# ScalarE alone reads the first layer's banks, and VectorE squares the even tile in SBUF

## The chip, the cores and the metric

The kernel runs on one core of a Trainium2 chip. The core has a matrix engine (TensorE, PE in the profile; its weight loads are listed as PEld), three engines for elementwise work (VectorE or DVE, ScalarE or ACT, GpSimd or POOL) and SyncE (SP), which here only issues DMAs. Matrix results land in PSUM, 8 banks of 128 partitions by 512 float32 values; everything else lies in SBUF. Each engine runs its own instructions in the order in which they were written and waits on semaphores that the others raise. The metric is the time of one execution on the device in microseconds (us), the median of several runs.

## The reference

Three layers follow one another. The first filters each of 8 batches (3072 by 256) in the frequency domain; the second is a feed-forward layer with a squared ReLU, 256 to 2048 to 256; the third is a soft mixture of 8 experts, of which every slot's input is a softmax over all 24576 tokens.

```python
y = np.fft.irfft(np.fft.rfft(x, axis=1) * F, n=x.shape[1], axis=1)   # per batch

h = np.maximum(x @ w_in, 0.0)
x = h * h @ w_out

logits = x @ phi
d = softmax over tokens of logits;  slot_input = d.T @ x
slot_out[e] = np.maximum(slot_input[e] @ w1[e], 0.0) @ w2[e]
out = (softmax over slots of logits) @ slot_out
```

The term that this case is about is `h * h` with `h = max(x @ w_in, 0)`: 24576 by 2048 values, computed in 768 tiles of 128 by 512.

## The kernel before

All weights of the first layer stay in SBUF, split in a high and a low part (`wiH`, `wiL`). The 24576 tokens go through in 48 chunks of 512 (`CH`), and each chunk's 2048 features in 8 pairs of 128-feature tiles, so the main loop has 384 pairs, P = 0 to 383. A pair has an even tile (k = 0, PSUM bank `p0`) and an odd tile (k = 1, bank `p1`). `layer` writes a tile with six matmuls (lines 382 to 384, twice): the three products of a split multiplication, for two halves of the inner dimension. There is one bank of each kind, so the first matmul of the next pair's even tile cannot begin before whoever reads `p0` is done with it; the same holds for `p1`.

`square` takes a tile from PSUM and leaves its squared ReLU in an SBUF tile `h` (tags `h0` and `h1`, four buffers each). The two kinds of tile go different ways. For the even tile ScalarE writes a scaled ReLU to `h` (line 390) and VectorE then reads the bank a second time and multiplies, `max(p, 0) * h` (line 391). [...]

VectorE then transposes each tile in blocks of 32 (`turn_h`, line 401, into `hT`), and PE multiplies `h` of four tiles by the product of the second layer's weights and `phi` into the chunk's logits in bank `L` (`logit`, line 410, called for P - 3 at each odd P). When a chunk's logits are complete, a chain runs beside the pairs of the following chunk. ScalarE and VectorE move the logits to SBUF (`evac_l`, lines 447 and 448), PE spreads them (`gather`, lines 455 and 456, bank X), VectorE takes the maximum (`emax`, lines 461 to 464), ScalarE the exponential (`expo`, line 470), VectorE transposes that into `eT` (`turn_e`, line 487) and the logits into `lt` (`turn_l`, line 481, four instructions), and PE then adds the chunk to the slots (`slot_in`, line 508, 128 matmuls into four banks), which VectorE accumulates (`accum`, line 524).

The frequency filter of the next batch is woven into the same loop: matmuls `mm_a` (lines 142 to 144), `mm_b` (188) and `mm_g` (221); between the last two VectorE multiplies by the filter (`filt`, line 199, four instructions) and GpSimd joins the parts (`join`, line 208, four instructions). GpSimd also makes the low parts of split tiles (lines 131 and 348).

The order on every engine is the order in which the Python code is called. `pair` emits one pair, and between its quarters `run_streams` calls those side steps whose due time has come and for which enough of the five side banks are free. `side` takes the bank that has been free the longest, and `done` puts a bank back at the end of that list. Nothing is reordered later; semaphores between engines are put in for every true dependence and every reuse of a buffer.

Of the kernel before, what the change touches and what calls it, by code (L numbers as in the profile page):

```python
# [9 lines left out]
ACTF = mybir.ActivationFunctionType  # L10
ALU = mybir.AluOpType
# [27 lines left out]
def body(tc, x, cA, cAf, fwd, inv, flt, cst, w_in, w_out, phi, w1, w2, out):  # L39
    nc = tc.nc  # L40
    sync = nc.sync
    act, vec, gps, pe = nc.scalar, nc.vector, nc.gpsimd, nc.tensor
# [343 lines left out]
    def square(P, k):  # L386
        p = h2[P, k]
        h = h2[P, k] = G["mlp"].tile([128, CH], F32, tag=f"h{k}", name="h", bufs=4)
        if k == 0:
            act.activation(out=h, in_=p, func=ACTF.Relu, scale=2.0 ** -16)  # L390
            vec.scalar_tensor_tensor(out=h, in0=p, scalar=0.0, in1=h, op0=ALU.max, op1=ALU.mult)  # L391
        else:
            act.activation(out=h, in_=p, func=ACTF.Relu, scale=2.0 ** -8)  # L393
            gps.tensor_tensor(out=h, in0=h, in1=h, op=ALU.mult)  # L394

    def turn_h(P, k):

# [17 lines left out]
    def pair(P):  # L415
        live = P < NP
        for k in range(4):
            t = 2 * P + 0.5 * k
            run_streams(t, True)
            if live:  # L420
                layer(P, k // 2, k % 2)
                if k % 2:
                    square(P, k // 2)
                if P % 8 == 7 and k == 3:
                    del xo[P // 8]
            if k == 2 and live:
                turn_h(P, 0)
            if k == 3 and 0 < P <= NP:
                turn_h(P - 1, 1)
            if k == 1 and P % 2 and P > 2:  # L430
                logit(P - 3)
            run_streams(t)
# [331 lines left out]
    with tc.manual_schedule():  # L764
# [77 lines left out]
        def bank(tag):  # L842
            return G["ps"].tile([128, 512], F32, tag=tag, name="pt")
# [74 lines left out]
        p = bank("s0")  # L918
# [8 lines left out]
        p = bank("s1")  # L927
# [31 lines left out]
        def layer2(r, h):  # L959
# [30 lines left out]
        p = bank("s4")  # L990
# [6 lines left out]
            out=sr[64:128], in0=p[64:128, 0:D], in1=sr[64:128].bitcast(F32), op=ALU.subtract  # L997
# [6 lines left out]
        for g in range(NG):  # L1004
# [4 lines left out]
            for h in range(2):  # L1009
                p = bank(("s0", "s1", "s2", "s3")[ops % 4]).rearrange("p (a d) -> p a d", d=D)  # L1010
# [156 lines left out]
```

## Time and profile before

| What | us |
|---|---|
| median of 3 runs | 2091.43 (2090.82 to 2091.57) |
| the profiled execution, its own time | 2097.94 |
| its span, from the first to the last instruction | 2096.2 |
| TensorE busy in the span | 2016.6 (96%) |
| VectorE busy | 1400.7 (67%) |
| ScalarE busy | 886.0 (42%) |
| GpSimd busy | 852.3 (41%) |

Busy times are unions of records. Matmuls are pipelined: in a full stream a new one starts every 0.23 us while each record lasts about 0.40 us. So records of PE overlap, and its pace is read from the distance between starts; the weight load of the next matmul is issued while the one before it still streams. "Idle before" a row is the time for which the engine had no record, with the instruction whose semaphore ended it behind the arrow.

### The profile page before, as it was taken

To read this page: it belongs to the slowest core of one execution; us is meant where nothing else is said; L and a number is where in the kernel's file an instruction comes from. 1 tells how busy PE (TensorE), PEld (TensorE's weight loads), DVE (VectorE), ACT (ScalarE), POOL (GpSimd) and SP (SyncE) were. 2 spreads that over 40 slices of the span, in tenths; PEclk is the share of its full clock that TensorE was granted. 3 is DMA by queue.
4 is the path that set the end of the run, shared out by engine and by line. 5 is a ranking of instruction groups with operands and counts; after the bars stand their busy time and mean duration, and the time that the engine had idled before them with its cause. 6 is when DMAs were issued, how large, how long until landed. Compare 5 with 4: busy or idle time off the path is not lost.

```text
span 2096.2 us, 44762 instructions
## 1 busy us (share of the span) xinstructions
PE 2016.6 (96%) x18334; PEld 1286.6 (61%) x18334; DVE 1400.7 (67%) x2564; ACT 886.0 (42%) x1780; POOL 852.3 (41%) x882
## 2 busy tenths in 40 slices
PE   6799999999999999999999999999999999999987
PEld 3376656666666666666666666566666666666556
DVE  3675766667667666667667666666666766666648
ACT  2345445344543345344543345334534344343335
POOL 2425454344534354344534354334534333232224
PEclk7699999999999999999999999999999999999989
DMA  9744454224333234224333234213423314000669
GB/s 283 211 144 133 106 170 132 71 67 112 109 85 98 71 112 133 71 63 117 107 82 101 72 108 137 71 42 105 133 79 94 90 45 144 15 22 14 185 227 384
DMA packets 145181, 238.31 MB, mean 114 GB/s; under 512 B 14800, under 2 KB 97232, under 8 KB 144976
## 3 DMA queue, kind: packets, MB, share of 16 engines
q1 hardware_dynamic: 144688, 235.25, 38.0%
q8 instruction: 144, 2.36, 0.5%
q14 instruction: 61, 0.50, 0.1%
q0 software_dynamic: 288, 0.20, 0.0%
HBM read 154.65 MB, written 80.74 MB: 112 GB/s over the span
## 4 chain that ended last, share of the span: by engine, by line
PE 86%; DVE 8%; DMA 2%; issue 2%; ACT 1%; SPq 0%; POOL 0%; DVEq 0%; ACTq 0%; POOLq 0%
PE p L382 19%; PE p L384 16%; PE p L383 16%; PE sd L508 10%; PE L L410 9%; PE sd L322 4%; PE sd L221 3%; DVE u L199 2%; PE sd L188 2%; DVE hT L401 1%; PE sd L142 1%; PE sd L143 1%; PE sd L144 1%; DVE ct L869 1%; PE pt L858 1%
## 5 line engine op out<-in xcount | busy, mean ns | idle before, releaser
L394 POOL TENSOR_TENSOR h<-h 128x512 f32<-128x512 f32 x384 | 401.6, 1046 | 890.6 <-ACT h L393 809.2
L382 PE MATMUL p<-xo,wiH 128*128 128x512 f32 x1536 | 653.5, 425 | 18.0 <-DVE h L391 14.4
L383 PE MATMUL p<-xo,wiH 128*128 128x512 f32 x1536 | 607.4, 395 | 0.9 <-POOL xo L348 0.9
L384 PE MATMUL p<-xo,wiL 128*128 128x512 f32 x1536 | 607.8, 396 | 0.0
L391 DVE SCALAR_TENSOR_TENSOR h<-p,h 128x512 f32<-128x512 f32 x384 | 265.1, 690 | 439.1 <-ACT h L390 437.6
L401 DVE STREAM_TRANSPOSE hT<-h 128x512 f32<-128x512 f32 x768 | 512.9, 694 | 12.2 <-POOL h L394 1.8
L393 ACT ACTIVATE h<-p 128x512 f32<-128x512 f32 x384 | 230.2, 599 | 527.5 <-PE p L384 525.2
L382 PEld LDWEIGHTS p<-xo,wiH 128*128 128x128 f32 x1536 | 288.9, 188 | 250.1 <-DVE h L391 86.0
L390 ACT ACTIVATE h<-p 128x512 f32<-128x512 f32 x384 | 229.7, 598 | 260.0 <-PE p L384 255.3
L384 PEld LDWEIGHTS p<-xo,wiL 128*128 128x128 f32 x1536 | 289.1, 188 | 69.6
L383 PEld LDWEIGHTS p<-xo,wiH 128*128 128x128 f32 x1536 | 290.0, 189 | 50.2 <-POOL xo L348 1.2
L208 POOL TENSOR_TENSOR u<-u 128x256 f32<-128x256 f32 x256 | 185.1, 747 | 174.6 <-DVE u L199 172.1
L508 PE MATMUL sd<-hT,eT 32*32 32x512 f32 x6144 | 219.8, 605 | 5.6 <-DVE eT L487 2.9
L410 PE MATMUL L<-h,wf 128*32 128x512 f32 x1536 | 205.6, 605 | 0.8 <-POOL h L394 0.8
L199 DVE TENSOR_TENSOR u<-sd,f 128x512 f32<-128x512 f32 x256 | 161.6, 675 | 36.5 <-PE sd L188 36.4
L524 DVE SCALAR_TENSOR_TENSOR ac<-ac,sc,sd 128x512 f32<-128x512 f32 x188 | 134.0, 734 | 67.6 <-PE sd L508 67.6
L508 PEld LDWEIGHTS sd<-hT,eT 32*32 32x32 f32 x6144 | 103.2, 103 | 117.5 <-issue 66.1
L131 POOL TENSOR_TENSOR u<-f,u 128x512 fp32r<-128x512 f32 x84 | 108.8, 1299 | 47.1 <-ACT u L130 37.5
L348 POOL TENSOR_TENSOR xo<-xt,xo 128x512 fp32r<-128x512 f32 x95 | 122.2, 1300 | 6.3 <-ACT xo L345 6.3
L332 ACT ACTIVATE xt<-sd 128x512 f32<-128x512 f32 x96 | 57.3, 597 | 142.5 <-PE sd L322 142.5
L230 ACT ACTIVATE f<-sd 128x256 f32<-128x256 f32 x256 | 79.8, 387 | 87.8 <-PE sd L221 87.8
L322 PEld LDWEIGHTS sd<-cst_t,gin 128*128 128x128 f32 x768 | 100.4, 191 | 9.4 <-DMA gin<-G 1.1
(111 smaller groups left out, 1598.3 us busy)
## 6 DMA issues: line engine op xcount, KB each, us to landing
f<-flt SPq DMA_DIRECT2D x64, 512.0 KB, 6.3
f<-x SPq DMA_DIRECT2D x48, 512.0 KB, 5.1
S<-u SPq DMA_DIRECT2D x96, 256.0 KB, 2.3
f<-S SPq DMA_DIRECT2D x128, 192.0 KB, 6.1
G<-f SPq DMA_DIRECT2D x128, 192.0 KB, 2.9
gin<-G SPq DMA_DIRECT2D x48, 512.0 KB, 5.4
out<-w1t SPq DMA_DIRECT2D x47, 512.0 KB, 5.1
wx<-w SPq DMA_DIRECT2D x34, 256.0 KB, 5.3
```

The costliest lines, as they stand in the source:

```text
L199: vec.tensor_tensor(out=u, in0=p.rearrange("p (h d) -> p h d", d=D), in1=f[:, 2 * r + k:2 * r + k + 1, :].to_broadcast([128, 2, D]), op=AL ...
L208: gps.tensor_tensor(out=a[:, h, :], in0=a[:, h, :], in1=b[:, 1 - h, :], op=ALU.add if h else ALU.subtract)
L382: pe.matmul(p, wh, x[:, 0, kk, :], start=(kk == 0), stop=False)
L383: pe.matmul(p, wh, x[:, 1, kk, :], start=False, stop=False)
L384: pe.matmul(p, wl, x[:, 0, kk, :], start=False, stop=(kk == 1))
L390: act.activation(out=h, in_=p, func=ACTF.Relu, scale=2.0 ** -16)
L391: vec.scalar_tensor_tensor(out=h, in0=p, scalar=0.0, in1=h, op0=ALU.max, op1=ALU.mult)
L393: act.activation(out=h, in_=p, func=ACTF.Relu, scale=2.0 ** -8)
L394: gps.tensor_tensor(out=h, in0=h, in1=h, op=ALU.mult)
L401: vec.transpose(hT[c][:, 2 * i + k, :], h2[P, k])
L410: pe.matmul(lg[c][32 * n:32 * n + 32, :], wf[:, f, :], h2.pop((P + n // 2, n % 2)), start=(f < 4), stop=(f >= FT - 4), tile_position=(0, 3 ...
L508: pe.matmul(S[r][32 * t:32 * t + 32, :], e[rows, o:o + 32], h[rows, :, o:o + 32], start=(a == 0), stop=(a == 3), tile_position=(32 * r, 32 ...
```

## The change

In `square` both tiles now go the same way. ScalarE writes the scaled ReLU of either bank to `h`, and the multiplication of `h` by itself is done in SBUF, by VectorE for the even tile and by GpSimd for the odd one. VectorE no longer reads `p0`. The scale of the even tile's ReLU becomes that of the odd one, which gives the same product.

```diff
     def square(P, k):
         p = h2[P, k]
         h = h2[P, k] = G["mlp"].tile([128, CH], F32, tag=f"h{k}", name="h", bufs=4)
-        if k == 0:
-            act.activation(out=h, in_=p, func=ACTF.Relu, scale=2.0 ** -16)
-            vec.scalar_tensor_tensor(out=h, in0=p, scalar=0.0, in1=h, op0=ALU.max, op1=ALU.mult)
-        else:
-            act.activation(out=h, in_=p, func=ACTF.Relu, scale=2.0 ** -8)
-            gps.tensor_tensor(out=h, in0=h, in1=h, op=ALU.mult)
+        act.activation(out=h, in_=p, func=ACTF.Relu, scale=2.0 ** -8)
+        (vec, gps)[k].tensor_tensor(out=h, in0=h, in1=h, op=ALU.mult)
```

No instruction moves on any engine; in 384 places one VectorE instruction is replaced by another. What changes beside it is who waits for whom. In the rows below, on PE, somewhere in the second batch, the bank `p0` is written anew by the first L382 that carries a wait; in square brackets stands the engine whose semaphore it waits for. Before:

```order
L144 MATMUL sd<-u,ca_t 128x512 [waits Pool_49]
L382 MATMUL p<-xo,wiH 128x512
L383 MATMUL p<-xo,wiH 128x512
L384 MATMUL p<-xo,wiL 128x512
L382 MATMUL p<-xo,wiH 128x512 [waits DVE_49]
L383 MATMUL p<-xo,wiH 128x512
```

And at the same place of the changed kernel:

```order
L144 MATMUL sd<-u,ca_t 128x512 [waits Pool_49]
L382 MATMUL p<-xo,wiH 128x512
L383 MATMUL p<-xo,wiH 128x512
L384 MATMUL p<-xo,wiL 128x512
L382 MATMUL p<-xo,wiH 128x512 [waits Activation_49]
L383 MATMUL p<-xo,wiH 128x512
```

The wait for VectorE has become a wait for ScalarE. The other place on PE is the logits, which read the squared tiles. Before, the wait at `p0` had already covered VectorE's part of them:

```order
L384 MATMUL p<-xo,wiL 128x512
L410 MATMUL L<-h,wf 32x512 x4
L382 MATMUL p<-xo,wiH 128x512 [waits Activation_49]
L383 MATMUL p<-xo,wiH 128x512
L384 MATMUL p<-xo,wiL 128x512
```

In the changed kernel (where the line of the logits is L406) the logits carry waits for VectorE of their own:

```order
L384 MATMUL p<-xo,wiL 128x512
L406 MATMUL L<-h,wf 32x512 [waits DVE_49]
L406 MATMUL L<-h,wf 32x512
L406 MATMUL L<-h,wf 32x512 [waits DVE_49]
L406 MATMUL L<-h,wf 32x512
```

Nothing stands in another order there; two waits are new.

## Rows read from the trace of the kernel before

**Rows 1.** The page: busy time by engine; the chain that ended last.

```profile
PE 2016.6 (96%) x18334; PEld 1286.6 (61%) x18334; DVE 1400.7 (67%) x2564; ACT 886.0 (42%) x1780; POOL 852.3 (41%) x882
...
PE 86%; DVE 8%; DMA 2%; issue 2%; ACT 1%; SPq 0%; POOL 0%; DVEq 0%; ACTq 0%; POOLq 0%
```

**Rows 2.** Groups by line: shapes, count | busy us, mean ns | idle before, releasers.

```profile
L382 PE MATMUL p<-xo,wiH 128*128 128x512 f32 x1536 | 653.5, 425 | 18.0 <-DVE h L391 14.4 <-ACT xo L345 1.2
...
L383 PE MATMUL p<-xo,wiH 128*128 128x512 f32 x1536 | 607.4, 395 | 0.9 <-POOL xo L348 0.9
...
L391 DVE SCALAR_TENSOR_TENSOR h<-p,h 128x512 f32<-128x512 f32 x384 | 265.1, 690 | 439.1 <-ACT h L390 437.6
...
L613 DVE TENSOR_TENSOR wa<-wa,we 128x512 f32<-128x512 f32 x8 | 5.5, 692 | 0.3
```

**Rows 3.** Waits of the span: us in total, times, longest us.

```profile
PEld p L382 <- DVE h L391: 86.0, 160, 1.3
...
PEld sd L508 <- DVE lt L481: 21.8, 26, 0.8
```

**Rows 4.** Timeline around one wait at the bank: start us, us, engine, [idle before].

```profile
641.51 0.40 PE L384 MATMUL p<-xo,wiL 128*128 128x512 f32 x1
...
641.95 0.60 ACT L390 ACTIVATE h<-p 128x512 f32<-128x512 f32 x1 [1.25 <-PE p L384]
...
642.58 0.69 DVE L391 SCALAR_TENSOR_TENSOR h<-p,h 128x512 f32<-128x512 f32 x1 [0.25 <-ACT h L390]
...
642.91 0.40 PE L384 MATMUL p<-xo,wiL 128*128 128x512 f32 x1
...
643.32 0.19 PEld L382 LDWEIGHTS p<-xo,wiH 128*128 128x128 f32 x1 [0.45 <-DVE h L391]
643.32 0.50 PE L382 MATMUL p<-xo,wiH 128*128 128x512 f32 x1
...
643.66 0.40 PE L383 MATMUL p<-xo,wiH 128*128 128x512 f32 x1
...
643.89 0.40 PE L384 MATMUL p<-xo,wiL 128*128 128x512 f32 x1
...
643.94 0.67 DVE L487 STREAM_TRANSPOSE eT<-et 128x512 f32<-128x512 f32 x1
...
644.53 1.25 DVE L481 STREAM_TRANSPOSE lt<-sd 32x128 f32<-32x128 f32 x4
...
645.91 0.25 PEld L508 LDWEIGHTS sd<-hT,eT 32*32 32x32 f32 x32 [0.84 <-issue]
```

**Rows 5.** Timeline of a longer wait at the bank, one chunk earlier.

```profile
603.68 1.42 POOL L208 TENSOR_TENSOR u<-u 128x256 f32<-128x256 f32 x2
...
604.53 0.68 DVE L391 SCALAR_TENSOR_TENSOR h<-p,h 128x512 f32<-128x512 f32 x1
...
605.27 0.19 PEld L382 LDWEIGHTS p<-xo,wiH 128*128 128x128 f32 x1 [1.23 <-DVE h L391]
...
605.88 0.67 DVE L487 STREAM_TRANSPOSE eT<-et 128x512 f32<-128x512 f32 x1
...
607.86 0.25 PEld L508 LDWEIGHTS sd<-hT,eT 32*32 32x32 f32 x32 [0.84 <-DVE lt L481]
```

**Rows 6.** Timeline: two SBUF inputs on VectorE beside GpSimd.

```profile
128.17 1.58 POOL L394 TENSOR_TENSOR h<-h 128x512 f32<-128x512 f32 x1 [4.25 <-ACT h L393]
...
128.88 1.41 DVE L645 TENSOR_TENSOR wa<-wa,we 128x512 f32<-128x512 f32 x1
```

**Rows 7.** Timeline: GpSimd's queue ahead of one mm_g.

```profile
663.62 1.29 POOL L348 TENSOR_TENSOR xo<-xt,xo 128x512 fp32r<-128x512 f32 x1
...
664.86 1.45 POOL L208 TENSOR_TENSOR u<-u 128x256 f32<-128x256 f32 x2
...
667.25 0.67 PEld L221 LDWEIGHTS sd<-u,iv 32*64 32x64 f32 x32 [0.84 <-issue]
```

**Rows 8.** One batch: length; busy of PE, PEld, DVE, ACT, POOL; clock, DMA.

```profile
570.00:806.00 236.00, 233.31 (x2216) 149.41 (x2192) 160.74 (x296) 102.86 (x206) 101.99 (x105) 1.00 0.34 97
```

## The prediction

> **What bounds the kernel.** I read the page's busy times and its chain first. TensorE is busy for 96% of the span and holds 86% of the chain; VectorE comes next with 67% and 8% [rows 1]. In a steady batch PE is busy for 233 of 236 us at a granted clock of 1.00 [rows 8], so a faster side engine alone buys nothing; a gain must shorten PE's own time. Second I looked in the table by line for PE time that is no work. L382 and L383 do the same matmul, yet L382's mean is 425 ns and L383's 395, and VectorE's L391 ended 14.4 of the 18.0 us for which PE had no record before L382 [rows 2]. Third, the list of waits names it: the weight load of L382 waited for L391 160 times, 86.0 us in all [rows 3]. That is the write to `p0` by the next pair.
>
> Fourth, the timeline shows what one such wait is [rows 4]. The last matmul of the even tile starts at 641.51, ScalarE reads the bank from 641.95 to 642.55, VectorE again from 642.58 to 643.27, and only then, at 643.32, do the next weights load. Without a wait the three matmuls of the odd tile's second half would be followed at once: L384 at 642.91, two steps of 0.23 later L383 at 643.37. It starts at 643.66, so the wait costs 0.28 to 0.29 us where the list counts a gap of 0.45. The difference, 0.17, is time in which PE still streamed. The whole cost of these waits is then 86.0 - 160 x 0.17 = 58.8 us. I added up the same thing from the starts of matmuls on either side of every such wait and got 59.0.
>
> **What the change removes.** `p0` comes free at the end of ScalarE's read. In [rows 4] that is 642.55, or 0.77 ahead of the weight load at 643.32, and the load would have been due 0.41 ahead of it (a gap of 0.04 instead of 0.45), at 642.91. A release takes 0.05 (643.27 to 643.32), so the bank would be ready at 642.60, 0.31 before it is needed. The longest waits, 1.23 [rows 5], come from a VectorE that is late, not from ScalarE, and go too. `p1` has worked that way all along, behind ScalarE only, and no wait for L393 stands among those of L382. I checked it for the case that PE no longer pauses: with each pause taken out, the odd tile's bank is late in 13 places, by 0.01 us each. So ScalarE's side costs nothing, and what is removed is 58.8 us.
>
> **What it adds on VectorE.** 384 instructions with a PSUM and an SBUF input, 690 ns each, become 384 with SBUF inputs. The nearest row for these is L613, two SBUF inputs of the same size, 692 ns [rows 2]: no difference.
>
> [...]
>
> What does differ is how VectorE then stands beside GpSimd. Two instructions show it [rows 6]. L645 has two SBUF inputs. It starts at 128.88, while GpSimd's L394 runs until 129.75, and takes 1.41 instead of 0.69: its end is GpSimd's end plus 0.54. L394 itself took 1.58 there instead of its usual 1.04. So these two do not run side by side. An even-tile square that begins with R us of a GpSimd instruction left ends R - 0.15 later than it would (0.69 - 0.54), and a GpSimd instruction can lose 0.54 behind a VectorE one. L391 shows nothing of the kind today, with a single SBUF input.
>
> [...]
>
> How often? GpSimd is busy for 102 of 236 us in instructions of about 0.97 us (102 / 105) [rows 8]. If the two engines met at random, 43% of 384 squares would find half an instruction left, R = 0.49, and lose 0.34: 56 us of VectorE time. VectorE has 33% to spare, so only the places count where PE waits for it.
>
> The first is the chain from `gather` to `slot_in`. Of 48 chunks 18 look like the one in [rows 5] (every second or third one, chunks 5 to 39). There the square at 604.53 meets two L208 on GpSimd that run until 605.10, R = 0.57: it ends 0.42 later, and so do the transposes behind it, `eT` at 606.97 instead of 606.55. PE, which no longer loses 1.23 - 0.17 = 1.06, comes to L508 at 607.86 - 1.06 = 606.80 and waits until about 607.04: 0.24 given back, 18 x 0.24 = 4.3 us. In chunks like that of [rows 4] GpSimd is idle when the square starts, `eT` ends at 644.61, 1.30 before L508, and after the change still 1.0 before it: nothing is given back.
>
> The second is the join on GpSimd ahead of `mm_g`. There it ends at 666.31, 0.94 before L221 [rows 7]. GpSimd's L348 holds until 664.91, the square of 663.91 slips in behind it and sets L208 back by 0.54, and PE comes 0.28 earlier: 0.12 is left, and 0.05 of it is the release. I count 1.5 us for the twelve or so places of this kind. The other `mm_g` of a batch have 1.4 us and more to spare. The new waits at the logits cost nothing: they ask for a square three pairs old.
>
> **Sum.** 58.8 - 4.3 - 1.5 = 53.0 us. The profiled execution took 2097.94 us, span 2096.2; without 53.0 the span is 2043.2. Its own time lies 6.5 us above the median of the runs, so the median becomes 2091.43 - 53.0 = 2038.4 us. For the lock's cost the ends are: nothing, 2033 (58.8 off), and all of the 56 us on PE's path, 2089. I stay near the first because the timeline fixes who meets whom.
>
> **Rivals.**
> The gain halves. The list of waits says that L508 waited for `lt`, 26 times [rows 3], and `lt` ends at 645.78, 0.13 before L508 [rows 4]. If that wait is real, PE would come early and stand at `slot_in` for what it saved since `gather`. 45 of the waits lie in such stretches: 18 of 1.06, 21 of 0.28 and 6 of 0.17, together 26.0 us, of which 0.08 each (3.6) stays; and the 18 late squares cost their full 0.42, 7.6. Left: 58.8 - 26.0 + 3.6 - 7.6 - 1.5 = 27.3, or 2064 us. For it speaks that the 0.13 returns in chunk after chunk. Against it: `side` hands out the oldest of five banks, and `lt`'s bank was given back last; followed through the code, only 7 of 48 chunks reuse it in `slot_in`, as the last of four. The 0.13 has a plainer cause: PE and VectorE both restart at the end of L391.
>
> Nothing is gained. The random meetings of the two engines, 56 us, come out on PE's path through filter, join and accumulation. 2091.43 - 58.8 + 56 = 2089 us. VectorE's third of idle time speaks against it.
>
> Slower. GpSimd falls behind ahead of `mm_g`. Each of its instructions there (L394, L348, two L208) is held up once by 0.54, 2.2 us in all; less the 0.94 of [rows 7], that is 1.22 for each of 56 `mm_g`, 68 us: 2091.43 - 58.8 + 68 = 2101 us. The mechanism decides from 1.05 us a place. For it speaks the 1.58 of [rows 6]; against it that most squares start when GpSimd is idle, as in [rows 4], and that most `mm_g` have more to spare.
>
> **How the numbers follow.** Forecast 0.64 (its own range 2032 to 2050), halved gain 0.20 (2054 to 2074), nothing gained 0.09 (2080 to 2095), slower 0.07. The range 2031 to 2072 holds the first and nearly all of the second. A measurement of this kernel can tell 0.2%, 4 us, from no change; on that count faster has 0.64 + 0.20 + 0.04 = 0.88, the same 0.06 (0.05 of the third case, 0.01 of the last), slower 0.06.
>
> **What would show it.** Right: no wait of L382 for the square's engine, L382's mean near L383's, the square itself longer than 0.69 in some 170 of 384 places and never shorter, PE's 53 us found at the end of the span. L508 keeps a wait, for `eT`, of some 0.2 us in 18 chunks. Wrong: waits of L382 for ScalarE in numbers, L508 standing a full 0.2 to 1 us for `lt`, or L221 waiting for L208 over 1 us at a time.

## The result, and the profile after

The changed kernel takes 2040.91 us (median of 4 runs, 2039.44 to 2042.45); the kernel before took 2091.12 in the 4 runs beside it. The ratio is 0.9764, 95% interval 0.9747 to 0.9781: 50.2 us or 2.4% faster. The forecast was 2038.4 us.

| | before | after |
|---|---|---|
| span of the profiled execution, us | 2096.2 | 2038.1 |
| TensorE busy, us | 2016.6 | 1965.6 |
| VectorE busy, us | 1400.7 | 1501.4 |
| GpSimd busy, us | 852.3 | 896.0 |

The page of the changed kernel, busy time by engine, and one batch from its list of windows (length; busy of PE, PEld, DVE, ACT and POOL; granted clock, DMA share, GB/s), which answer to [rows 1] and [rows 8]:

```profile
PE 1965.6 (96%) x18334; PEld 1292.4 (63%) x18334; DVE 1501.4 (74%) x2564; ACT 882.7 (43%) x1780; POOL 896.0 (44%) x882
```

```profile
559.00:787.90 228.90, 228.03 (x2193) 151.02 (x2192) 174.75 (x296) 102.06 (x207) 108.11 (x105) 1.00 0.35 99
```

PE is as busy as before in a kernel that is shorter, and two side engines are busier: time left PE, not VectorE. The same batch as that of [rows 8] now takes 228.9 us instead of 236, with VectorE busy for 175 instead of 161 of them. The groups by line (count | busy us, mean ns | idle before):

```profile
L390 POOL TENSOR_TENSOR h<-h 128x512 f32<-128x512 f32 x384 | 406.8, 1059 | 816.3 <-ACT h L389 739.8
L382 PE MATMUL p<-xo,wiH 128*128 128x512 f32 x1536 | 636.4, 414 | 1.2 <-ACT xo L345 1.2
L390 DVE TENSOR_TENSOR h<-h 128x512 f32<-128x512 f32 x384 | 376.4, 980 | 339.2 <-ACT h L389 338.7
...
L208 POOL TENSOR_TENSOR u<-u 128x256 f32<-128x256 f32 x256 | 201.7, 810 | 155.8 <-DVE u L199 153.3
```

Beside [rows 2]: the idle time before L382 that L391 had ended is gone, and the mean falls from 425 to 414 ns. VectorE's square takes 980 ns on average where 690 had stood. In the list of waits (us in total, times, longest) no line has L382 wait for VectorE any more. The prediction took waits of L382 for ScalarE in numbers as a sign of being wrong. There are 43 where there were 38, and 36 of them are of 0.84 us in either kernel:

```profile
PEld p L382 <- ACT h L390: 31.0, 38, 0.8
```

```profile
PEld p L382 <- ACT h L389: 32.9, 43, 0.8
```

The first line is of the kernel before, the second of the changed one. What PE waits for around `slot_in` and `mm_g` is now:

```profile
PEld sd L504 <- DVE eT L483: 20.9, 18, 1.2
...
PEld sd L221 <- POOL u L208: 15.4, 17, 2.9
...
PE sd L504 <- DVE eT L483: 7.6, 20, 2.9
...
PE sd L221 <- POOL u L208: 5.7, 6, 2.4
```

The place of [rows 4] in the changed kernel's timeline (start us, us, engine, [idle before]):

```profile
630.25 0.40 PE L384 MATMUL p<-xo,wiL 128*128 128x512 f32 x1
...
630.69 0.60 ACT L389 ACTIVATE h<-p 128x512 f32<-128x512 f32 x1 [1.27 <-PE p L384]
...
631.32 0.69 DVE L390 TENSOR_TENSOR h<-h 128x512 f32<-128x512 f32 x1 [0.25 <-ACT h L389]
...
631.65 0.40 PE L384 MATMUL p<-xo,wiL 128*128 128x512 f32 x1
631.65 0.19 PEld L382 LDWEIGHTS p<-xo,wiH 128*128 128x128 f32 x1
...
632.12 0.40 PE L383 MATMUL p<-xo,wiH 128*128 128x512 f32 x1
...
632.68 0.67 DVE L483 STREAM_TRANSPOSE eT<-et 128x512 f32<-128x512 f32 x1
...
633.27 1.25 DVE L477 STREAM_TRANSPOSE lt<-sd 32x128 f32<-32x128 f32 x4
...
634.37 0.25 PEld L504 LDWEIGHTS sd<-hT,eT 32*32 32x32 f32 x32 [0.84 <-issue]
```

The bank's weights load at 631.65, 0.36 behind ScalarE's end (631.29) and while VectorE is still busy with the square. L383 follows L384 by 0.47, two steps, where it had been 0.75. `slot_in` starts 1.02 behind the end of `eT` (633.35) and 0.15 ahead of the end of `lt` (634.52).

The place of [rows 5], the longer wait:

```profile
594.07 1.43 POOL L208 TENSOR_TENSOR u<-u 128x256 f32<-128x256 f32 x2
...
594.40 0.19 PEld L382 LDWEIGHTS p<-xo,wiH 128*128 128x128 f32 x1
...
594.93 1.12 DVE L390 TENSOR_TENSOR h<-h 128x512 f32<-128x512 f32 x1
...
596.72 0.67 DVE L483 STREAM_TRANSPOSE eT<-et 128x512 f32<-128x512 f32 x1
597.31 0.91 DVE L477 STREAM_TRANSPOSE lt<-sd 32x128 f32<-32x128 f32 x3
597.44 0.24 PEld L504 LDWEIGHTS sd<-hT,eT 32*32 32x32 f32 x32 [1.16 <-DVE eT L483]
```

No gap before the weights at 594.40. The square meets the second L208 and takes 1.12 instead of 0.69; it ends 0.55 behind GpSimd (595.50). `eT` ends at 597.39 and `slot_in` starts 0.05 later with a gap of 1.16 instead of the usual 0.84: the wait that was forecast, 0.3 instead of 0.24 long, in 18 chunks.

I summed the distances between starts of matmuls, before and after, by what each matmul does. L382 and L383 together take 59.8 us less (58.8 forecast), `slot_in` 4.1 more (4.3), `mm_g` 1.6 more (1.5); the rest of the kernel's 58.1 us between the two spans, 4 us less, is spread over its beginning and its end.

Place by place the last two do not agree with the forecast. In the 18 chunks that it named `slot_in` takes 5.8 us more, 0.32 each; all other chunks together take 1.7 less. Of that 0.8 is a pause of PE inside one `slot_in`, in another chunk of either trace, for which the profile names no releaser (the first row is of the kernel before):

```profile
1361.23 1.92 PE L508 MATMUL sd<-hT,eT 32*32 32x512 f32 x6 [2.71 <-issue]
```

```profile
1401.69 1.68 PE L504 MATMUL sd<-hT,eT 32*32 32x512 f32 x6 [2.13 <-issue]
```

Of the 63 places of `mm_g` the 48 from 380 us on take 1.27 us each, before and after: they pay nothing. The 1.6 us come from the first 15, in the first 320 us, and a second trace of the changed kernel (the run of 2042.48 us below) has 2.9 us less there than the first, so 1.3 less than before. Only two of the 15 take more in both traces, by 0.44 and 0.28 us.

### The profile page after: what moved, and what is told of

It reads as the page before. It is cut to its first block, busy times and chain, and to the rows that moved or that the text cites. A ratio compares the mean times of both kernels' runs of the same rounds, so it can differ in the third digit from the quotient of the medians.

```text
span 2038.1 us, 44827 instructions
## 1 busy us (share of the span) xinstructions
PE 1965.6 (96%) x18334; PEld 1292.4 (63%) x18334; DVE 1501.4 (74%) x2564; ACT 882.7 (43%) x1780; POOL 896.0 (44%) x882
## 4 chain that ended last, share of the span: by engine, by line
PE 84%; DVE 9%; issue 3%; DMA 2%; ACT 1%; SPq 1%; POOL 0%; DVEq 0%; ACTq 0%; POOLq 0%
PE p L382 17%; PE p L384 16%; PE p L383 15%; PE sd L504 11%; PE L L406 8%; PE sd L322 4%; PE sd L221 3%; DVE u L199 2%; PE sd L188 2%; DVE hT L397 2%; PE sd L142 1%; DVE h L390 1%; PE sd L143 1%; PE sd L144 1%; DVE ct L865 1%
## 5 line engine op out<-in xcount | busy, mean ns | idle before, releaser
L390 POOL TENSOR_TENSOR h<-h 128x512 f32<-128x512 f32 x384 | 406.8, 1059 | 816.3 <-ACT h L389 739.8
L382 PE MATMUL p<-xo,wiH 128*128 128x512 f32 x1536 | 636.4, 414 | 1.2 <-ACT xo L345 1.2
L390 DVE TENSOR_TENSOR h<-h 128x512 f32<-128x512 f32 x384 | 376.4, 980 | 339.2 <-ACT h L389 338.7
L383 PE MATMUL p<-xo,wiH 128*128 128x512 f32 x1536 | 607.1, 395 | 0.9 <-POOL xo L348 0.9
L384 PE MATMUL p<-xo,wiL 128*128 128x512 f32 x1536 | 607.3, 395 | 0.1
L382 PEld LDWEIGHTS p<-xo,wiH 128*128 128x128 f32 x1536 | 288.8, 188 | 171.7 <-issue 66.4
L384 PEld LDWEIGHTS p<-xo,wiL 128*128 128x128 f32 x1536 | 288.8, 188 | 69.7
L383 PEld LDWEIGHTS p<-xo,wiH 128*128 128x128 f32 x1536 | 289.4, 188 | 57.2 <-POOL xo L348 1.2
L208 POOL TENSOR_TENSOR u<-u 128x256 f32<-128x256 f32 x256 | 201.7, 810 | 155.8 <-DVE u L199 153.3
L406 PE MATMUL L<-h,wf 128*32 128x512 f32 x1536 | 205.6, 605 | 0.8 <-POOL h L390 0.8
L131 POOL TENSOR_TENSOR u<-f,u 128x512 fp32r<-128x512 f32 x84 | 118.5, 1415 | 42.6 <-ACT u L130 33.3
L348 POOL TENSOR_TENSOR xo<-xt,xo 128x512 fp32r<-128x512 f32 x95 | 133.6, 1419 | 6.6 <-ACT xo L345 6.5
L322 PE MATMUL sd<-cst_t,gin 128*128 128x128 f32 x768 | 101.1, 275 | 1.0 <-DMA gin<-G 1.0
```

The lines of the kernel that those rows point to most:

```text
L208: gps.tensor_tensor(out=a[:, h, :], in0=a[:, h, :], in1=b[:, 1 - h, :], op=ALU.add if h else ALU.subtract)
L322: pe.matmul(p[:, 128 * a:128 * a + 128], t[:, a, 128 * k:128 * k + 128], cI, start=True, stop=True,)
L382: pe.matmul(p, wh, x[:, 0, kk, :], start=(kk == 0), stop=False)
L383: pe.matmul(p, wh, x[:, 1, kk, :], start=False, stop=False)
L384: pe.matmul(p, wl, x[:, 0, kk, :], start=False, stop=(kk == 1))
L390: (vec, gps)[k].tensor_tensor(out=h, in0=h, in1=h, op=ALU.mult)
```

## The experiments

All but one, the changed kernel again, change the lines of `square` in the changed kernel. Times are medians; ratios are to the kernel before on the same chip, with the 95% interval. PE's times are the sums of distances between starts, against the changed kernel's trace.

**VectorE holds the bank again, but briefly.**

```diff
         act.activation(out=h, in_=p, func=ACTF.Relu, scale=2.0 ** -8)
+        if k == 0:
+            vec.tensor_copy(G["dsp"].tile([128, 1], F32, tag="jk", name="jk", bufs=2), p[:, 0:1])
         (vec, gps)[k].tensor_tensor(out=h, in0=h, in1=h, op=ALU.mult)
```

> The changed kernel, with one more VectorE instruction for the even tile, ahead of the square: a copy of a single column of p0 into a scratch tile, so that VectorE again is the last to let go of the bank, but after some 0.2 us instead of 0.69 and ahead of any meeting with GpSimd. My theory (the gain is the time between ScalarE's end and the bank's release, 0.31 us of which were to spare): the common waits of 0.28 us stay away, only those come back where VectorE is late for the bank, 18 places of about 0.55 us and a few more behind delayed squares; 2050 to 2065 us. Rival, that any use of the bank by VectorE costs what it did: about 2091 us.

2048.61 us, ratio 0.9807 (0.9785 to 0.9828). The group of the copy and the waits at the bank in this kernel:

```profile
L391 DVE COPY jk<-p 128x1 f32<-128x1 f32 x384 | 59.6, 155 | 336.4 <-ACT h L389 334.5
```

```profile
PEld p L382 <- DVE jk L391: 13.0, 18, 0.7
...
PE p L382 <- DVE jk L391: 5.2, 18, 0.3
```

Exactly the 18 places came back where VectorE is late; of the 142 others none. A VectorE that lets go of the bank after 0.16 us costs nothing where it is free. The time is 1.4 us below my range: PE lost 11.0 us at the bank, but 5.7 us less in the 18 chunks of `slot_in`, which again take what they took before the change, since a PE that has paused at the bank no longer comes too early for `eT`. I had not set the one against the other.

**VectorE holds the bank until the square is done.** The same copy, one line lower:

```diff
         (vec, gps)[k].tensor_tensor(out=h, in0=h, in1=h, op=ALU.mult)
+        if k == 0:
+            vec.tensor_copy(G["dsp"].tile([128, 1], F32, tag="jk", name="jk", bufs=2), p[:, 0:1])
```

> The same copy of one column of p0, but behind the square: VectorE lets go of the bank after the square and after any wait for GpSimd. Nothing else differs from the changed kernel; ScalarE still reads the whole bank and the square is still made in SBUF. My theory: every wait of the kernel before comes back, 0.2 us longer each (some 140 of 0.5, 18 of 1.3 and more), and now the square's waits for GpSimd, 111 us in the changed kernel's trace, reach PE wherever the bank is wanted; 2110 to 2200 us, slower than the kernel before. Rival, that the gain comes from the instruction (SBUF instead of PSUM) and not from the release: at most 2055 us.

2166.42 us, ratio 1.0367 (1.0348 to 1.0386): slower than the kernel before. Two waits of this kernel, whose square and ScalarE's work are the changed kernel's to the letter:

```profile
PE p L382 <- DVE jk L392: 87.3, 140, 1.4
...
PEld sd L506 <- DVE lt L479: 21.8, 26, 0.8
```

The second line is a trap and stands below as well. L382 and L383 take 133 us more than in the changed kernel. So the gain is the release of the bank, and the SBUF form of the square is of no use by itself: with the bank still behind it, the kernel is slower than before. How much of that loss is the copy itself, 0.15 us behind each square, and how much the square's waits for GpSimd, I did not separate.

**No even square at all.** The even tile stays unsquared, so this run shows what VectorE's squares cost and is no version of the kernel.

```diff
-        (vec, gps)[k].tensor_tensor(out=h, in0=h, in1=h, op=ALU.mult)
+        if k:
+            gps.tensor_tensor(out=h, in0=h, in1=h, op=ALU.mult)
```

> The changed kernel without VectorE's square: the even tile stays unsquared (this part of the computation is left out). VectorE loses 376 us of work and GpSimd no longer meets it there. My theory, that PE pays for the squares only at slot_in (4.1 us) and mm_g (1.6 us): 2033 to 2038 us. Rival, that VectorE's load and its 111 us of waits for GpSimd are the next bound: 2000 to 2020 us.

2029.9 us, ratio 0.9705 (0.9683 to 0.9726). The page's busy times:

```profile
PE 1965.9 (97%) x18334; PEld 1295.3 (64%) x18334; DVE 1154.3 (57%) x2180; ACT 881.6 (43%) x1780; POOL 851.4 (42%) x882
```

347 us less on VectorE and 45 on GpSimd are worth some 11 us. That is 3 us more than I expected, and far from the rival's 20 to 40. `slot_in` takes 9.8 us less than in the changed kernel, `mm_g` 4.5. Of the 9.8 the 18 chunks give 5.7: each is back at 4.40 us, as before the change. Another 3.3 is the pause inside one `slot_in`, which this execution does not have; the 4.5 stand in the first 15 places of `mm_g`, which differ by 2.9 between two traces of the same kernel. So 5.7 us are shown to be the squares' price; where the rest of the 11 us comes from stays open.

**GpSimd squares both tiles.**

```diff
-        (vec, gps)[k].tensor_tensor(out=h, in0=h, in1=h, op=ALU.mult)
+        gps.tensor_tensor(out=h, in0=h, in1=h, op=ALU.mult)
```

> GpSimd squares both tiles; VectorE's squares are gone and with them their meetings with GpSimd, while GpSimd gets 384 more instructions of 1.04 us (some 1250 us busy, 61%). My theory: slot_in no longer waits (4 us less), but each join stands behind one more 1.04 us, where 0.2 to 0.8 us is to spare at most of the 48 regular mm_g: 10 to 30 us more; 2045 to 2065 us. Rival, that the meetings are what counts: 2010 to 2030 us.

2047.98 us, ratio 0.9793 (0.9771 to 0.9815), within my range but not for my reason. Its waits:

```profile
DVE hT L397 <- POOL h L390: 631.8, 248, 6.6
...
PEld sd L504 <- DVE eT L483: 35.8, 26, 1.6
```

I had expected the joins to hold up the 48 regular `mm_g`, and each of them takes 1.27 us here too. `slot_in` took 6.7 us more than in the changed kernel, 8.2 more in the 18 chunks. VectorE has no square there, but the transpose of the even tile waits for GpSimd, and behind it, in VectorE's queue, stands `eT`. A meeting of two instructions was exchanged for a true wait in the same chain.

**The tile next to the chain alone.** Three edits of one kind, and the changed kernel again on the same chip. In the third pair of a chunk the even tile is squared by GpSimd:

```diff
-        (vec, gps)[k].tensor_tensor(out=h, in0=h, in1=h, op=ALU.mult)
+        (vec, gps)[k or P % 8 == 2].tensor_tensor(out=h, in0=h, in1=h, op=ALU.mult)
```

> As changed, but in the third pair of each chunk (P mod 8 = 2, the one between gather and slot_in) GpSimd squares the even tile too. VectorE's chain to eT loses a square and its wait for GpSimd there. Rival: slot_in's wait goes, 4 to 9 us faster than the changed kernel, 2032 to 2037 us. My theory, since GpSimd's run with both squares showed VectorE's transposes waiting for GpSimd 632 us: the transpose of that tile stands in the same chain, and GpSimd's square ends 1 us later than VectorE's would, so eT comes later; 2045 to 2060 us.

2049.48 us, ratio 0.9805 (0.9791 to 0.9818); the changed kernel beside it took 2042.48, ratio 0.9769 (0.9756 to 0.9782). What it was expected of:

> The changed kernel once more, so that the three others can be compared with it on the same chip: 2037 to 2044 us by either theory.

Slower by 7 us, as the transpose's wait had it; the 18 chunks of `slot_in` take 8.3 us more:

```profile
DVE hT L397 <- POOL h L390: 67.2, 61, 1.7
...
PEld sd L504 <- DVE eT L483: 35.0, 25, 1.6
```

The same tile by ScalarE:

```diff
-        (vec, gps)[k].tensor_tensor(out=h, in0=h, in1=h, op=ALU.mult)
+        if k == 0 and P % 8 == 2:
+            act.activation(out=h, in_=h, func=ACTF.Square)
+        else:
+            (vec, gps)[k].tensor_tensor(out=h, in0=h, in1=h, op=ALU.mult)
```

> As changed, but in the third pair of each chunk ScalarE squares the even tile, in the 0.9 us that it is idle between that tile's ReLU and the exponential. VectorE's chain to eT becomes shorter by 0.69 us, in 18 chunks by 0.42 more. My theory: slot_in's waits go, PE gets 4 us and up to 8 back, and nothing else changes; 2032 to 2037 us. Rival, that slot_in is not held by that square: as the changed kernel, 2040 to 2042 us.

2032.69 us, ratio 0.9725 (0.9711 to 0.9738): 9.8 us below the changed kernel, by 48 instructions on an engine that was idle there. Its group by line and what is left of the wait:

```profile
L391 ACT ACTIVATE h<-h 128x512 f32<-128x512 f32 x48 | 30.3, 632 | 1.5
```

```profile
PEld sd L507 <- DVE eT L486: 15.1, 18, 0.8
```

The 18 gaps are the usual 0.84 again. PE's `slot_in` time is 7.3 us less, 5.7 of it in the 18 chunks. The rest of the 9.8 us I have not traced to a place.

**ScalarE squares every even tile.**

```diff
-        (vec, gps)[k].tensor_tensor(out=h, in0=h, in1=h, op=ALU.mult)
+        if k == 0:
+            act.activation(out=h, in_=h, func=ACTF.Square)
+        else:
+            gps.tensor_tensor(out=h, in0=h, in1=h, op=ALU.mult)
```

> ScalarE squares the even tile itself, with a second instruction from SBUF to SBUF right behind its ReLU; VectorE has no square and meets no GpSimd there. ScalarE gets some 384 x 0.6 = 230 us more (54% busy). Its read of the odd bank now stands behind the square: 0.2 us are left between the two in a pair without other work on ScalarE. My theory (PE pays for whoever is late for a bank or for eT): the 9 to 11 us that the run without any even square showed are gained, and p1 comes late where ScalarE has other work in between, some 50 to 100 times by 0.2 to 0.3 us; 2032 to 2058 us. Rival, that VectorE's load and its waits for GpSimd alone are what is left to gain: 2030 us, as without the square.

2030.88 us, ratio 0.971 (0.9696 to 0.9725): the lowest median of the versions that compute the whole result, 0.6% below the changed kernel beside it and level with the run without any even square; its interval overlaps that of the version before it. Page and waits:

```profile
PE 1967.8 (97%) x18334; PEld 1296.5 (64%) x18334; DVE 1163.7 (57%) x2180; ACT 1109.8 (55%) x2164; POOL 852.1 (42%) x882
```

```profile
DVE hT L400 <- ACT h L391: 464.6, 225, 5.6
...
PEld p L382 <- ACT h L391: 1.9, 5, 0.4
```

My fear was wrong: the odd bank, read behind the square, was late in no numbers: 5 short gaps instead of 50 to 100 waits, and the changed kernel has gaps of the same 0.4 us in the same five places, put down there to the ReLU. Why ScalarE's other work does not collide with the two banks more often I did not test. VectorE's transposes wait 465 us for ScalarE in all, and yet `slot_in` takes 6.4 us less than in the changed kernel (5.7 in the 18 chunks): VectorE, busy for 57%, has the time.

## Why the prediction was right

**The bank.** Forecast 58.8 us, found 59.8. The two runs with a copy of one column show the mechanism: same square, same ScalarE, and the place where VectorE last touches the bank decides between 2049 and 2166 us. That ScalarE's side would cost nothing held too: its release left 0.31 us, and PE's weights load 0.36 behind its end.

**The meetings with GpSimd.** The form of the cost was right, the sum too small: the assumption of random meetings failed. 171 squares of 384 are longer than 0.72 us (some 170 forecast), none is shorter (651 ns at the least, 654 before), and most of them end 0.545 to 0.555 behind the end of the GpSimd instruction that they met (0.54 in [rows 6]). That the count agrees is partly chance: by the forecast's own R - 0.15, meetings at random would have left an estimated 25 of its 165 squares (43% of 384) at 0.69, those that find less than 0.15 of the 0.97 us left. And the squares lose 111 us in all, where random meetings gave 56. A good part of the difference lies in squares that begin just behind a GpSimd instruction, two of the trace's rows here:

```profile
615.18 2.99 POOL L348 TENSOR_TENSOR xo<-xt,xo 128x512 fp32r<-128x512 f32 x2
615.20 1.81 DVE L390 TENSOR_TENSOR h<-h 128x512 f32<-128x512 f32 x1 [3.10 <-ACT h L389]
```

GpSimd's queue is full; it ends a square at 615.22 and the next instruction is on its way at 615.18, 0.02 ahead of VectorE's. VectorE waits for the whole of it, 1.81 instead of 0.69, and the second L348 then waits for VectorE (2.99 for two of 1.29). In 32 places the square takes over 1.75, some 35 of the 111 us. The estimate of random meetings gave each of them half an instruction. The other 139 lose 0.54 each where 0.34 was reckoned; why they too begin early in a GpSimd instruction I did not test.

**Where PE pays for it.** At `slot_in` the mechanism is the one forecast, in the same 18 chunks, and its term was too small: 5.8 us against 4.3. At `mm_g` the forecast's 1.5 us did not come in any of the 48 regular places; at most 0.7 us, in two of the first 15, is the change's. The two misses cancel nearly, which is luck. That 111 us of VectorE's and 44 of GpSimd's time came to no more than some 6 us is not luck: both had it to spare elsewhere. The place of [rows 7]:

```profile
653.06 1.88 POOL L208 TENSOR_TENSOR u<-u 128x256 f32<-128x256 f32 x2
...
655.16 0.66 PEld L221 LDWEIGHTS sd<-u,iv 32*64 32x64 f32 x32 [0.84 <-DVE hT L397]
```

The first L208 takes 0.44 longer behind the square, and the join ends 0.22 ahead of `mm_g` (0.12 forecast, 0.94 before). The gap is the usual 0.84, so the name behind its arrow tells nothing.

**The rival that the gain halves** fell with the first trace: `slot_in` begins before `lt` is done, by 0.15 us in chunks like [rows 4] and by 1.1 in the 18 others. Its evidence was the list of waits. The experiment that put the bank back behind VectorE shows the same "26 times, 21.8 us for `lt`" again, in a kernel where the same weight load does not need it: two events that both follow the release of the bank, 0.13 apart, look like a wait. What told them apart was the list of free banks in the code.

**Nothing gained, or slower.** Neither came. GpSimd's delay ahead of `mm_g` was 0.44 once at the place of [rows 7], not four times 0.54. The waits of over 1 us for L208 that the list still has at `mm_g` (2.9 at most, 1.9 before) all stand in the first 320 us.

**The time itself.** 2040.9 against 2038.4. On PE the forecast's 53.0 was 54.0 (59.8 less 5.8); between the medians it is 50.2. The two profiled executions differ by 58, since that of before was 6.5 us above its median and that of after 0.8 below. A mere shift of the median by PE's time carries that much error, 3 to 8 us here.

## What to carry to other kernels

When a single PSUM bank passes between TensorE and its readers, what counted here is the last reader's end (2049 against 2166 us with the same square): take the bank's contents out once, with the engine that is first at hand, and do the rest in SBUF, even by an instruction that is no shorter (0.69 us for VectorE's square in either form, 0.98 on average with what it lost to GpSimd). Before crediting such a gain, follow PE to the next thing it needs and see how much earlier that is ready; here the spare 1.3 us before `slot_in` held nearly all of it. Where the moved work then shares VectorE with a chain that PE waits for, an engine without that chain behind it is the better place (here ScalarE, 55% busy: 2031 against 2042 us).

## What the runs showed of the hardware

Where VectorE's square and a GpSimd instruction met, what each lost was not always the same. The square with two SBUF inputs took VectorE 0.65 to 1.82 us: over 1.75 in 32 places, where it began 0.01 to 0.12 us behind a GpSimd instruction, and 0.69 where it began 0.08 ahead of one:

```profile
272.57 0.69 DVE L390 TENSOR_TENSOR h<-h 128x512 f32<-128x512 f32 x1 [0.52 <-ACT h L389]
272.65 1.52 POOL L390 TENSOR_TENSOR h<-h 128x512 f32<-128x512 f32 x1
```

GpSimd lost some 0.4 to 0.5 us at a time behind VectorE's square, here 1.52 against its usual 1.04.

ScalarE's square from SBUF took 632 ns, against 597 for its ReLU from PSUM in the same run, and changing between Relu, Copy, Exp and Square 384 times loaded no further table: ScalarE has 2164 instructions there, the changed kernel's 1780 and the 384 squares, and of those 1780 a single one is a table load, of 1.28 us, at 0.74 us.
